# A new instruction list for the first third of a chunked-scan layer followed by a squared-ReLU FFN, on one core

## The chip, the cores and the metric

The kernel runs on one core of a Trainium2 chip. The core has a matrix engine (PE in the profile, with its weight loads shown as PEld), a vector engine (DVE), a scalar engine (ACT), a general engine (POOL, also called GpSimd) and a queue engine that only issues transfers (SP). ACT and POOL issue transfers too. The metric is the device time of one execution in microseconds (us).

## The reference

The program is a gated linear recurrence over a sequence, and then a feed-forward network (FFN) on its output. There are 4 batches, 8 heads, 768 tokens, head width 32 and state width 16.

```python
log_a = np.log(np.clip(a, 1e-06, 1.0))
for c in range(nc):                       # chunks of tokens
    cum = np.cumsum(la, axis=-1)
    L = np.exp(cum[:, :, :, None] - cum[:, :, None, :]) * causal
    M = np.einsum('bhin,bhjn->bhij', Cc, Bc) * L
    y_intra = np.einsum('bhij,bhjd->bhid', M, xc)
    y_inter = np.einsum('bhin,bhnd->bhid', Cc, state) * np.exp(cum)[:, :, :, None]
    y[:, :, sl] = y_intra + y_inter
    state = decay_full[:, :, None, None] * state + np.sum(Bx, axis=2)
x = y.transpose(0, 2, 1, 3).reshape(B * S, H * D)      # 3072 x 256
h = np.maximum(x @ w_in, 0.0)                          # 256 -> 2048
out = (h * h) @ w_out                                  # 2048 -> 256
```

## The kernel before

**Units and blocks.** The kernel replaces the chunks of 32 tokens by chunks of 128 and works on 12 units of 256 tokens each (two chunks): units 0 to 3 are the first third of the four batches, 4 to 7 the second, 8 to 11 the last. The decays are not taken as exponents of sums but as running products: `P` is the running product of `a`, C is multiplied with P, and x with 1/P, so that a causal mask of zeros and ones is all that is left of the decay matrix. Each unit becomes one FFN block of 256 tokens; the blocks are called a to l.

**Everything is ordered by hand.** The string `ORDER` is a list of short names, and the function `one` (line 655) issues what each name stands for. The framework adds the semaphores; it does not reorder. So the place of a name in the list fixes the order of the instructions on each engine, and each engine works through its own instructions in that order. The FFN uses PSUM banks of 2 KB, which `bank` (line 352) hands out in rotation among those not marked busy.

**The names**, with k the unit:

- `fa0`, `fa1`, `la`: loads of `a`. `ldB`, `ldC`, `ldx`: loads of B, C and x of a unit (l and h are the two halves of the heads), with the issuing queue behind the colon (s for SP, a for ACT). `ld4` and so on load all three. `wi0` to `wi3` and `wo0` to `wo3` load a quarter of w_in and w_out each from POOL's queue, 512 KB in the memory, converted on the way.
- `id2:512`: idle products, here two of 128x512, of ones with ones, whose results nobody reads.
- `wm`: a first small copy on ACT, ahead of which the function table is loaded (line 487). `ku ef eb ti pi` build masks and identities on POOL, `jz` clears a buffer for B and C, `mb` builds the causal mask, `hd` and `pk` prepare a small product.
- `sk` (clip and running product of the first third of `a`), `sp` (its transposition on PE), `ps`, `iv1` and `iv` (copy and reciprocals), `su`, `to`, `fq` (the decay totals). `sn`, `p2` and `pq` are the same for the other two thirds of `a`; `sn` is three DVE instructions (lines 468, 469, 532).
- `pc`, `pb`: C times P, and B, into the buffer `jt`. `px`: x times 1/P into `xs`. `tr` and `tc`: transposition of `jt` on PE and copies out of PSUM (units 0 to 3; from unit 4 on a transposing transfer from SP). `mt`: the scores of a unit, into banks 0 to 3.
- `mk`: mask one bank of scores straight from PSUM on DVE (line 229). `sc` and `ms`: copy a bank by ACT (line 234) and mask the copy on DVE or POOL (line 238). A unit has four such steps. `u`: the unit's addition to the state, `us` its copy, `sf` the first state of a unit (line 343), `za zb sa sb` the later states.
- `in`, `ina`, `inb`: products of the masked scores with x. `ca`: product with the state. `t`: copy of the result to `T`, the input of the block (two copies; aa is ACT twice, vv DVE twice).
- `a0` to `a7`: the eight up-products of block a (line 403, four products of 128x256 each), followed by a ReLU on ACT (line 408). `qa0`: the square on DVE (line 414). `A0` to `A7`: the down-products (line 430). The same with b and B, and so on.
- `rg4`: state products, additions and scores of two neighbouring units together, from the middle of the list on. `bk` and `fr` release banks. `gB3`, `gx3`: a memset on POOL that a later load has to wait for.

**Around the change.** The list falls into a front (up to `rg4`) and a steady part, in which up- and down-products alternate and one unit is prepared per block. The diff touches the front of the list and functions that it calls.

Of the kernel before, what the change touches and what calls it, by code (L numbers as in the profile page):

```python
# [30 lines left out]
def kernel(  # L31
# [180 lines left out]
    T = {}  # L212
# [14 lines left out]

    def ph_mask(k, q):
        nc.vector.tensor_tensor(out=live[k]["mts"][:, q].rearrange("p r g i -> p (r g i)"),  # L229
                                in0=pp[:, q, :], in1=mask, op=ALU.mult)  # L230

    def ph_score(k, q):
        sc = big.tile([128, 512], BF16, tag="sc", name=f"sc{k}_{q}")
        nc.scalar.copy(out=sc, in_=pp[:, q, :])
        live[k].setdefault("sc", {})[q] = sc

    def ph_mask_sb(k, q, eng):
        eng.tensor_tensor(out=live[k]["mts"][:, q].rearrange("p r g i -> p (r g i)"),  # L238
                          in0=live[k]["sc"][q], in1=mask, op=ALU.mult)
# [8 lines left out]
    def ph_carry(k, h, begun):  # L248
        for i in range(2):
# [18 lines left out]
    def ph_intra(k, h, begun, qs=range(4)):  # L268
        v = live[k]
        for g in range(2):  # L270
# [8 lines left out]
    def ph_t(k, h, engs=None):  # L279
# [5 lines left out]
        for i, eng in enumerate(engs or (nc.scalar, nc.scalar)):  # L285
            copy(eng, _fap(T[k], i * 64, [[128, 4], [1, 64]]), _fap(pp, h[i] * 512, [[64, 4], [1, 64]]))

# [51 lines left out]
    def ph_sd_first(k):  # L339

        v, b = live[k], UNITS[k][0]
        S_d = spool.tile([128, 256], BF16, tag=f"Sd{b}0", name=f"Sd{k}_0")
        nc.vector.tensor_tensor(  # L343
# [7 lines left out]

    def bank():
        h = next(h for h in turn if h not in busy)
# [4 lines left out]
    def pair():  # L358
        free = sorted((turn.index(h), h) for h in turn if h not in busy)
# [36 lines left out]
    def mm1(blk, fp):  # L396

        h = bank()
        gi, o = group_of(WIN, fp)
        w = w_in_b[gi]  # L400
        for i in range(2):
            for g in range(2):
# [3 lines left out]
                                 start=(g == 0), stop=(g == 1), skip_group_check=True)  # L406
# [49 lines left out]
    with tc.manual_schedule():  # L456
# [131 lines left out]
        def scores(k):  # L588
# [3 lines left out]
            live[k]["todo"] = [0, 1, 2, 3]  # L592
            live[k]["copied"] = []
            live[k]["masked"] = []

        def mask_direct(k):
            q = live[k]["todo"].pop(0)
            ph_mask(k, q)
            busy.discard(q)
# [164 lines left out]
```

## Time and profile before

| | |
|---|---|
| median of three runs | 116.73 us (116.39 to 117.14) |
| the profiled execution | 116.84 us, of which the span of instructions is 115.1 us |
| PE busy | 108.9 us (95% of the span) |
| DVE, ACT, POOL busy | 84.2 us (73%), 76.7 us (67%), 49.8 us (43%) |
| memory read and written | 10.58 MB, 3.15 MB |

The profiled execution has 1.7 us around its span. Busy shares are means over the span; the first 17 us and the rest differ, so that the views by stretch, by time and by chain are read besides.

### The profile page before, as it was taken

Reading aid. Unit: us, or ns where it says so; the run is one execution under the profiler, and the core shown is the slowest. Engines: PE = TensorE matmul, PEld = TensorE weight load, DVE = VectorE, ACT = ScalarE, POOL = GpSimd, SP = SyncE. Lnnn points to the kernel's source line nnn. Section 1 sums busy time; section 2 is a strip of 40 time slices with the busy share of each in tenths; the row PEclk is TensorE's granted clock in tenths of the full one; section 3 lists DMA queues with packets and bytes.
Section 4 is the critical chain, followed back from the end, with each engine's and each line's share of the span. In section 5 each row is a group of like instructions: output and inputs, shape, how many; then the busy total and the mean of one; then the engine's idle time right before and its main releaser. Section 6 shows DMA issues by size and latency. Waiting matters only on the chain.

```text
span 115.1 us, 3998 instructions
## 1 busy us (share of the span) xinstructions
PE 108.9 (95%) x1623; PEld 93.5 (81%) x1623; DVE 84.2 (73%) x187; ACT 76.7 (67%) x161; POOL 49.8 (43%) x102
## 2 busy tenths in 40 slices
PE   7977969999999999999999999999999999999990
PEld 2344749978898989989989989989989899899980
DVE  2469996779599969969965989849668488445530
ACT  0655667865598756787486686786777776876840
POOL 7369972068599457548602669038020020000000
PEclk9999999999999999999999999999999999999999
DMA  1999999989999913935915926623023020020202
GB/s 29 199 196 145 199 203 189 215 167 210 180 191 211 214 24 108 160 89 155 179 46 122 178 97 123 132 95 73 0 100 68 0 100 0 6 91 0 91 0 91
DMA packets 47814, 13.46 MB, mean 117 GB/s; under 512 B 44276, under 2 KB 45876, under 8 KB 47796
## 3 DMA queue, kind: packets, MB, share of 16 engines
q1 hardware_dynamic: 43828, 10.64, 44.8%
q0 software_dynamic: 1664, 2.10, 10.8%
q10 hardware_dynamic: 2304, 0.48, 2.0%
q8 instruction: 12, 0.20, 0.8%
q14 instruction: 6, 0.05, 0.1%
HBM read 10.58 MB, written 3.15 MB: 119 GB/s over the span
## 4 chain that ended last, share of the span: by engine, by line
PE 87%; DMA 6%; POOL 2%; issue 1%; DVE 1%; ACT 1%; ACTq 0%; DVEq 0%
PE pp L430 36%; PE pp L403 36%; PE pp L245 6%; DMA w_out_b<-in_moe_w_out_dram 6%; PE pp L476 4%; PE pp L220 3%; POOL mts L238 1%; PE pp L195 1%; POOL jt L158 1%; PE pp L452 1%; DVE jt L158 0%; DVE Sd L343 0%; ACT bct L208 0%; PE pp L521 0%; ACT osl L722 0%
## 5 line engine op out<-in xcount | busy, mean ns | idle before, releaser
L408 ACT ACTIVATE hb<-pp 128x512 bf16<-128x512 f32 x96 | 55.0, 599 | 24.7 <-PE pp L403 23.1
L430 PE MATMUL pp<-w_out_b,h 128*128 128x256 bf16 (+1 forms) x400 | 54.3, 268 | 0.8 <-DMA w_out_b<-in_moe_w_out_dram 0.8
L414 DVE TENSOR_TENSOR h<-hb 128x512 bf16<-128x512 bf16 x96 | 45.0, 486 | 12.7 <-ACT hb L408 12.3
L403 PE MATMUL pp<-T,w_in_b 128*128 128x256 bf16 x384 | 54.2, 273 | 0.0
L403 PEld LDWEIGHTS <-w_in_b 128*128 128x128 bf16 x384 | 41.4, 114 | 2.2 <-issue 1.0
L430 PEld LDWEIGHTS <-h 128*128 128x128 bf16 x400 | 37.6, 98 | 5.4 <-DVE T L210 1.1
L229 DVE TENSOR_TENSOR mts<-pp,mask 128x512 bf16<-128x512 f32 x45 | 29.6, 677 | 3.3 <-PE pp L220 3.3
L331 POOL TENSOR_TENSOR Sd<-z,Pquad 128x256 bf16<-128x256 f32 x16 | 11.1, 693 | 32.9 <-DVE z L315 25.7
L177 POOL TENSOR_TENSOR xs<-x_nat,Pinv 128x256 bf16<-128x256 f32 (+1 forms) x19 | 14.4, 776 | 5.2 <-DVE Pinv L546 4.6
L158 POOL TENSOR_TENSOR jt<-C_nat,P_sb 128x128 bf16<-128x128 f32 x22 | 9.4, 449 | 1.5 <-ACT P_sb L688 1.0
L476 PE MATMUL pp<-const-bfloat16-1.0 128*128 128x512 bf16 (+2 forms) x19 | 7.3, 516 | 0.8 <-PEq L748 0.8
L315 DVE SCALAR_TENSOR_TENSOR z<-z,Ptot,us 128x64 f32<-128x64 f32 x8 | 2.2, 281 | 6.3 <-ACT us L299 5.4
L437 ACT COPY osb<-pp 128x512 f32<-128x512 f32 x11 | 6.3, 584 | 0.4 <-PE pp L430 0.4
L245 PE MATMUL pp<-mts,xs 64*32 64x128 bf16 x384 | 5.9, 219 | 0.1
L170 POOL CAST jt<-B_nat 128x128 bf16<-128x128 f32 x17 | 5.4, 341 | 1.4 <-DMA B_nat<-in_B_dram 1.4
L220 PE MATMUL pp<-bct 32*64 32x256 bf16 x192 | 5.1, 279 | 0.9 <-DVE bct L210 0.6
L476 PEld LDWEIGHTS <-const-bfloat16-1.0 128*128 128x128 bf16 x19 | 2.2, 122 | 4.0 <-issue 3.7
L245 PEld LDWEIGHTS <-xs 64*32 64x32 bf16 x384 | 4.2, 90 | 0.6 <-issue 0.4
L282 ACT CAST T<-pp 128x512 bf16<-128x512 f32 x7 | 4.1, 592 | 0.4 <-PE pp L245 0.2
L208 ACT CAST T<-pp 128x256 bf16<-128x256 f32 x8 | 2.6, 375 | 2.6 <-PE pp L245 2.6
L245 PE MATMUL pp<-bct,Sd 128*128 128x128 bf16 x40 | 4.2, 220 | 0.0
L220 PEld LDWEIGHTS <-bct 32*64 32x64 bf16 x192 | 2.1, 102 | 2.0 <-issue 0.6
(62 smaller groups left out, 53.4 us busy)
## 6 DMA issues: line engine op xcount, KB each, us to landing
x_nat<-in_x_dram SPq DMA_DIRECT2D x11, 256.0 KB, 3.7
out_dram<-osb SPq DMA_DIRECT2D x11, 256.0 KB, 3.2
B_nat<-in_B_dram SPq DMA_DIRECT2D x11, 128.0 KB, 3.1
C_nat<-in_C_dram SPq DMA_DIRECT2D x11, 128.0 KB, 3.4
w_in_b<-in_moe_w_in_dram POOLq DMA_DIRECT2D x4, 256.0 KB, 6.8
w_out_b<-in_moe_w_out_dram POOLq DMA_DIRECT2D x4, 256.0 KB, 8.2
x_nat<-in_x_dram ACTq DMA_DIRECT2D x2, 128.0 KB, 3.4
bct<-jt SPq DMA_TRANSPOSE x8, 3.6
```

The source lines that it names most:

```text
L158: eng.tensor_tensor(out=_fap(jt[k % 3], 128 + 144 * g, [[384, 2], [32, 4], [1, 16]]), in0=_fap(loaded[k]["C"], 128 * g, [[16, 2], [32, 4], ...
L177: eng.tensor_tensor(out=_fap(xs, 256 * r, [[256, 2 // n], [32, 8], [1, 32]]), in0=_fap(loaded[k]["x"], 32 * r, [[32, 2 // n], [64, 8], [1, ...
L220: nc.tensor.matmul(pp[64 * u:64 * u + 64, q, r * 256:r * 256 + 256], bct[32 * q:32 * q + 32, r, 0, u * 64:u * 64 + 64], _fap(bct[32 * q:32 ...
L229: nc.vector.tensor_tensor(out=live[k]["mts"][:, q].rearrange("p r g i -> p (r g i)"), in0=pp[:, q, :], in1=mask, op=ALU.mult)
L245: nc.tensor.matmul(dst, w, v, start=bool(need), stop=False, skip_group_check=True, **({} if pos is None else {"tile_position": pos}))
L331: nc.gpsimd.tensor_tensor(out=_fap(S_d, 0, [[128, 2], [32, 4], [1, 32]]), in0=_fap(z, 0, [[32, 2], [0, 4], [1, 32]]), in1=_fap(Pquad, 4 * ...
L403: nc.tensor.matmul(pp[:, h, i * 256:(i + 1) * 256], _fap(w, g * w.shape[2] + (o // 2) * 512 + 2 * (o % 2) + i, [[4, 128]]), T[blk][:, g].r ...
L408: nc.scalar.activation(out=hb.rearrange("p i t -> p (i t)"), in_=pp[:, h, :], func=AF.Relu)
L414: nc.vector.tensor_tensor(out=h2, in0=hb, in1=hb, op=ALU.mult)
L430: nc.tensor.matmul(dst, h2[:, i, r * 128:(r + 1) * 128], w_out_b[gi][:, 2 * o + i, c0:c1], start=first, stop=(fp == 7 and i == 1), skip_gr ...
L437: nc.scalar.copy(out=osb, in_=pp[:, 6 if blk == 1 else 7, :])
L476: nc.tensor.matmul(pp[:, h, 0:int(cols)], ones_b[:, 0:128], ones_b[:, 0:int(cols)] if dep is None else dep, start=True, stop=True, skip_gr ...
```

## The change

`ORDER` is rewritten from its start up to `rg4`; from there on it is the same. In the new front:

- the idle products ahead of the FFN are 28 instead of 19, with more of them between `sp` and the first `ca`, and of other sizes;
- on ACT, `wm` stands ahead of the loads of the lower halves of C and x of unit 0 (`ldC0:l`, `ldx0:l`), behind them before;
- `jz0` goes from DVE to POOL, `jz1` and `jz2` trade places, `pbl0` and `pbh0` trade engines (DVE and POOL for POOL and ACT);
- `in0` stands ahead of `mt1`; `sf0` and `sf2` are on ACT (four activations each) instead of DVE;
- POOL issues `wo0`, `wi2` and `wi3` ahead of `px1`; `px1` stood between `wo0` and `wi2`;
- after the masks of unit 1 come `sf1`, then `sn`; `p2` stands behind `a3`;
- four up-products of block b are issued ahead of `A0`; none before. Some up-products are issued in halves (`a0:0`, `a0:1`), each half two of the four products;
- on DVE instead of POOL or ACT: `pb2`, `px2`, `tc3:1`, `px4`, `pc5`, `pb5`; `t1` goes from DVE to ACT; unit 2 is masked by `mk` alone, unit 3 has one `sc` and `ms`; `pb3` goes from ACT to POOL;
- the gate `gx3` behind `wo2` replaces `gB3` at the start, and SP loads C of unit 2 ahead of B.

The tuple `HALF` is empty, so the branches for it aren't taken. The quarters of the weights stay as they were.

```diff
-        id3:512 fa1:a la fa0:s ku ef ldx0:h:a eb id2:512 ti id1:512 gB3 pi ldB0:l:a hd ldC0:l:a ldB0:h:s ldC0:h:s
-        ldx0:l:a wm jz0:v mb jz1:v ldB1:s id3:512 sk pbh0:a id2:512 pk pbl0:p wi0 sp pc0:v ldC1:s trB0 wi1 su iv1:0:8
-        trC0 tcC0:0:v tcB0:2:a id1:512 tcC0:1:a ps pb1:a to px0:v jz2:v mt0 id1:512 u0:67 ldx1:s pc1:p fq sc0 mk0
-        id1:512 mk0 ms0:p tr1 tc1:1:v sc0 tc1:0:a sf0 mt1 ldB2:s wo0 ldC2:s ms0:v ldx2:s id1:384 in0 ca0 iv:8:16
-        id3:512 px1:p t0:aa id1:256 mk1 a0 a1 mk1 mk1 mk1 u1 ina1 inb1 sn1 us0 sf1 qa0 a3 ldC3:s wi2 fr p2 wi3 ca1
-        qa1 wo1 pc2 pb2:a t1:vv us1 iv:32:64 a2 zb0 qa2 zb1 A0 ldB3:s wo2 ldx3:s b3 qb3 b0 pq b2 b1 tr2 wo3 sb1 qa3
-        qb0 A1 b5 b4 qb1 qb2 qb5 tc2:1:v qb4 tc2:0:a a5 B0 b6 B1 a7 qa5 iv:16:32 px2 a6 mt2 B3 A2 sc2 u2 b7 us2 pb3:a
-        pc3 mk2 qa6 px3 mk2 A5 ms2:v mk2 ld4 qb6 sf2 a4 qa7 B5 pc4 A6 A3 ld5 pb4 ina2 inb2 tr4 ca2 t2:aa tr3 B4 B2
-        tc3:0:a tc3:1:a u3:45 qb7 ld6 ld7 mt3 qa4 B6 mk3 mk3 mk3 mk3 us3 c4 c5 c0 A4 A7 B7 c6 qc0 za3 qc4 c1 qc5 qc6
-        sa3 px4 qc1 pc5 pb5 bk c2 rg4 tr5 C0 mk4 mk4 qc2 c7 qc7 sb0 c3 qc3 d2 d1 C5 za4 afC2 d0 C1 px5 C4 qd2 zb3 C6
+        la jz2:v fa1:a id1:384 id1:512 id2:512 jz0:p fa0:s ldB0:h:s id2:512 ldx0:h:a ldC0:h:s ku ef ldB0:l:a ti wm
+        id1:512 ldC0:l:a ldx0:l:a id2:512 sk id1:128 eb id1:128 sp mb pbl0:v hd id1:256 id1:384 id1:256 iv1:0:8 pi
+        pbh0:p ldB1:s id1:384 wi0 ldC1:s ps id1:512 ldx1:s trB0 pk jz1:v pc0:v tcB0:2:a id1:384 id1:128 su trC0
+        tcC0:0:a to iv:8:16 tcC0:1:v pb1:a id2:512 wi1 px0:v fq mt0 id2:512 ldC2:s pc1 sc0 sc0 mk0 id1:384 u0:67
+        id2:512 ms0:p mk0 wo0 wi2 wi3 ms0:v tr1 us0 ldB2:s in0 id1:128 px1:p tc1:0:a tc1:1:v mt1 id2:512 sf0:a ldx2:s
+        ca0 t0:aa a0:0 mk1 a0:1 mk1 ldC3:s mk1 mk1 a1 u1 sf1 us1 a2:0 a2:1 ina1 inb1 wo1 sn1 a3:0 ca1 t1:aa ldB3:s
+        a3:1 p2 b1:0 b2:0 b1:1 qa3 qa1 qa0 pc2:p b0 b3 iv:16:32 b2:1 qb1 A0 wo2 gx3 iv:32:64 ldx3:s zb1 fr qb0 a5 A1
+        b5 wo3 B0 pb2:v B1 b4:0 pq qa5 qb2 b4:1 a7:0 qb3 a6 pc3 pb3:p a7:1 tr2 tc2:1:a px2:v B3 b6 A3 qb4 qb5 tc2:0:v
+        B2 u2@45 mt2 qa2 A2 ld4 qa6 sb1 qa7 B5 us2 mk2 b7 px3:p mk2 sf2:a pc4 A5 mk2 a4 A6 mk2 tr3 ca2 ina2 inb2
+        tc3:0:a t2:aa tc3:1:v mt3 ld5 qb6 B4 pb4:p sc3 u3:45 qa4 qb7 B6 mk3 us3 c4 tr4 c0 px4:v mk3 ld6 B7 pc5:v za3
+        A4 qc4 mk3 ms3:v qc0 c6 sa3 c5 A7 pb5:v c1 bk zb0 ld7 qc5 c2 qc1 qc6 rg4 tr5 C0 mk4 mk4 qc2 c7 qc7 sb0 c3 qc3
...
-    def ph_sd_first(k):
+    def ph_sd_first(k, eng=None):
...
+        if eng is nc.scalar:
+            for q in range(4):
+                nc.scalar.activation(out=_fap(S_d, 32 * q, [[128, 2], [1, 32]]),
+                                     in_=_fap(pp, v["h"][0] * 512 + 256, [[32, 2], [1, 32]]),
+                                     func=AF.Copy, scale=Pquad[:, total(0, b, 0), q:q + 1])
+            v["S"] = [None, S_d]
+            return
...
+    def mm1(blk, fp, part=None):
+
+        h = opened.pop((blk, fp)) if part == 1 else bank()
...
-            for g in range(2):
+            for g in (0, 1) if part is None else (part,):
...
-                                 start=(g == 0), stop=(g == 1), skip_group_check=True)
+                                 start=(g == 0 and (part is None or i == 0)), stop=(g == 1), skip_group_check=True)
+        if part == 0:
+            opened[(blk, fp)] = h
+            busy.add(h)
+            return
+        busy.discard(h)
```

More of the change, by code (lines that the diff above doesn't have):

```diff
@@ L286, in ph_t, with ph_t_half @@
             copy(eng, _fap(T[k], i * 64, [[128, 4], [1, 64]]), _fap(pp, h[i] * 512, [[64, 4], [1, 64]]))
+    def ph_t_half(k, h, g, eng):
+        if k not in T:
+            T[k] = tpool.tile([128, 2, 2, 2, 64], BF16, tag="T", name=f"T{k}")
+        d = h[1] - h[0]
+        copy(eng, _fap(T[k], 256 * g, [[128, 2], [64, 2], [1, 64]]),
+             _fap(pp, h[0] * 512 + 128 * g, [[64, 2], [512 * d, 2], [1, 64]]))
     state = {}
@@ L350 @@
     busy = set()
+    forced = []
     def bank():
-        h = next(h for h in turn if h not in busy)
+        h = forced.pop(0) if forced else next(h for h in turn if h not in busy)
+        assert h not in busy
         turn.remove(h)
@@ L358, in pair @@
     def pair():
+        if forced:
+            return tuple(bank() for _ in range(2))
         free = sorted((turn.index(h), h) for h in turn if h not in busy)
@@ L591, in scores, with read_out @@
             busy.update(range(4))
-            live[k]["todo"] = [0, 1, 2, 3]
+            live[k]["todo"] = [(g, p) for g in range(2) for p in range(2)] if k in HALF else [0, 1, 2, 3]
             live[k]["copied"] = []
             live[k]["masked"] = []
+        def read_out(k, q):
+            if k not in HALF:
+                busy.discard(q)
+            elif q[0]:
+                busy.difference_update((2 * q[1], 2 * q[1] + 1))
         def mask_direct(k):
@@ L598, in mask_direct @@
             ph_mask(k, q)
[L599 removed]
+            read_out(k, q)
             live[k]["masked"].append(q)
@@ L622, in intra @@
             v = live[k]
+            if k in HALF:
+                gs = {"": (0, 1), "a": (0,), "b": (1,)}[part]
+                assert all((g, p) in v["masked"] for g in gs for p in range(2))
+                ph_intra(k, v["h"], v["begun"], range(4), gs)
+                return
             qs = v["masked"][{"": slice(0, 4), "a": slice(0, 2), "b": slice(2, 4)}[part]]
```

68 lines of the change are left out of this document (45 added, 23 removed).

## The prediction

> **What bounds the kernel now.** I read the chain of waits first, in order of time, then the busy time by stretch. The columns of the chain are start, length (us) and what it was.
>
> ```profile
> 0.85 4.85 PE pp L476 x11
> ...
> 10.33 6.49 DMA w_out_b<-in_moe_w_out_dram
> 16.82 0.14 issue
> 16.96 0.60 PE pp L430 x4
> 17.56 1.75 PE pp L403 x16
> ```
>
> ```profile
> 16.96:112.19 95.23, 95.10 (x1424) 86.01 (x1424) 72.07 (x156) 68.09 (x136) 37.16 (x70) 1.00 0.53 110
> 20.00:35.00 15.00, 14.88 (x241) 12.80 (x244) 12.13 (x25) 10.91 (x26) 9.22 (x18) 1.00 1.08 193
> ```
>
> The second fence has a stretch, its length, the busy time of PE, PEld, DVE, ACT and POOL, the granted clock, the DMA share and GB/s. From 16.96, where the first down-product A0 starts, to 112.19 PE is busy 95.10 of 95.23 us. So the kernel is a front of 17 us in which PE mostly waits, and then 95 us of PE work without a hole. What A0 waited for is the first quarter of w_out, issued at 10.33 and landed 6.49 us later. The time changes by two things alone: how early PE becomes dense, with how much useful work done before, and what holes the dense part gets or loses. One hole is there to lose:
>
> ```profile
> 26.35 1.47 PE L430 MATMUL pp<-w_out_b,h 128*128 128x256 bf16 x12
> 27.94 0.27 PE L245 MATMUL pp<-mts,xs 64*32 64x128 bf16 x5
> ```
>
> A product of 128x256 takes 1.75/16 = 0.109 us in a row, four of them 0.44 (one name such as `a0`). Twelve from 26.35 issue until 27.66; the next is at 27.94, so 0.28 us are lost.
>
> **The change part by part.** From `rg4` on the list is the same, and the useful PE work of the front is the same set. I walk the new front, with the durations of before.
>
> *Until the first scores.* The 11 first idle products now have 4736 columns instead of 5632. At the early rate (4.85/11 = 0.44 us for 512) they end at about 4.9 instead of 5.7. That gains nothing, as `sp` waits for the scan of `a`, and the transfer of `a` keeps its place. What moves is C:
>
> ```profile
> 2.44 0.53 ACTq L125 DMA_DIRECT2D C_nat<-in_C_dram  x1
> 3.01 0.52 ACTq L125 DMA_DIRECT2D x_nat<-in_x_dram  x1
> 3.56 1.28 ACT L487 ACT_TABLE_LOAD   x1 [3.56 <-issue]
> 4.85 0.19 ACT L487 COPY warm<-warm 128x2 bf16<-128x2 bf16 x1
> ```
>
> The table load and copy (1.28 + 0.19) now stand ahead of these two issues, so C's lower half is issued at 2.44 + 1.5 = 3.9, x's at 4.5: the first x is not moved up for this half, but back. The time from issue to landing of this C transfer was
>
> ```profile
> DMA to landing us min/median/max: 3.2/3.2/3.2
> ```
>
> and so it lands at 7.1 instead of 5.6. Below, the first products with C (6.31) did not wait for it; now they start at 7.1.
>
> ```profile
> 6.31 0.49 DVE L158 TENSOR_TENSOR jt<-C_nat,pp 128x128 bf16<-128x128 f32 x2 [0.96 <-PE pp L452]
> ...
> 7.77 0.68 DVE L177 TENSOR_TENSOR xs<-x_nat,Pinv 128x512 bf16<-128x512 f32 x1
> 8.48 0.38 DVE L685 MEMSET jt<- 128x384 uint32 x1
> ...
> 11.00 2.42 DVE L229 TENSOR_TENSOR mts<-pp,mask 128x512 bf16<-128x512 f32 x4
> 13.34 0.37 DVE L468 TENSOR_SCALAR a_cl<-a_nat 128x128 f32<-128x128 f32 x1
> 13.74 0.43 DVE L469 TENSOR_TENSOR_SCAN cp<-a_cl,const-float32-0.0 128x128 f32<-128x128 f32 x1
> 14.20 0.84 DVE L532 TENSOR_SCALAR pick_p<-pick,cp 128x16 f32<-128x16 f32 x1
> 14.96 0.41 DVE L343 TENSOR_TENSOR Sd<-pp,Pquad 128x256 bf16<-128x256 f32 x1
> ```
>
> ```profile
> 7.47 0.38 PE L476 MATMUL pp<-const-bfloat16-1.0 128*128 128x512 bf16 x1
> 8.09 0.42 PE L220 MATMUL pp<-bct 32*64 32x256 bf16 x16 [0.24 <-ACT bct L208]
> ```
>
> From those products to the scores (8.09) it took 1.78 us, with the reciprocal and `su` in between, which now come earlier. I take 1.5, so the scores of unit 0 start at 8.6, 0.5 late. The memset of `jt` (0.38), `pbl0` and `hd`, new on DVE ahead of the products with C, lie beside the wait for C; without it they would cost at most 0.4.
>
> *The idle products* between `sp` and `trC0` hold 2304 columns. At the early rate that is 4.5 x 0.44 = 1.98 us, at the later one 4.5 x 0.22 = 0.99 (twice 0.109 for 512 columns; the single one at 7.47 took 0.38 with its way through the array, where the early ones come every 0.44). They start at about 6.2 and are over at 7.2 or 8.2; `trC0` can start at 7.6. So they cost between 0 and 0.6. I take 0, as the rate was already the later one at 7.47, and keep 0.6 for the range. The granted clock is 1.00 in every row and does not show this. The Trainium skill, "TensorE: Matmul & The Clock Gate", Part 1, says that PE starts at half rate and is released after a window of about 3.4 us of sustained activity, a window that runs freely; by that rule the pause of the new list between 4.9 and 5.6 can fall into the window and put the release off, the idle products meant to keep the rate up would then run at half of it ahead of real work, and the sum would be 0.6 higher.
>
> *Masks, T and the products with x.* POOL is next:
>
> ```profile
> 8.24 0.82 POOL L158 TENSOR_TENSOR jt<-C_nat,P_sb 128x128 bf16<-128x128 f32 x2 [1.00 <-ACT P_sb L688]
> 9.04 0.23 POOL L527 TENSOR_TENSOR Pquad<-Ptot,quad 128x32 f32<-128x32 f32 x1
> 9.24 1.15 POOL L238 TENSOR_TENSOR mts<-sc,mask 128x512 bf16<-128x512 bf16 x1
> 10.33 0.60 POOL L143 DMA_DIRECT2D w_out_b<-in_moe_w_out_dram  x1
> 11.18 1.04 POOL L177 TENSOR_TENSOR xs<-x_nat,Pinv 128x512 bf16<-128x512 f32 x1 [0.24 <-DVE Pinv L546]
> 12.17 1.47 POOL L139 DMA_DIRECT2D w_in_b<-in_moe_w_in_dram  x2
> ```
>
> Its mask came 1.15 after the scores started and took 1.15: now 9.75 to 10.9. `in0` follows at 10.95, as before (10.94). `mt1` now stands behind `in0` and an idle product, at 11.35 instead of 10.31: 1.0 late. Its four masks (2.42) run from 11.8 to 14.2. Meanwhile POOL issues `wo0` (0.60) and `wi2`, `wi3` (1.47) from 10.9 to 13.0 and only then makes xs of unit 1 (1.04): 14.0, against 12.2 before. `u1` and `ina1`, on PE in order behind it, wait for 14.0 and 14.2; so both delays end together. `sf1` follows (0.41) to 14.7 or 14.9, then `sn`: from its first to the end of its last instruction 1.70 us (13.34 to 15.04), so 16.5, then the sums of `p2` on PE, and the first product of b at about 16.65. T1, copied by ACT after `ca1`, is there before. a0 to a3, units 0 and 1 and `p2` are then done: exactly what was done at 16.96. **PE gets dense 0.3 us earlier.** The four activations for `sf0` on ACT have no row; between 0.19 (the small copy) and 0.41 (the DVE instruction) each, they take 0.8 to 1.6. I take 0.8, hidden by the idle products ahead of `ca0`; at 1.6 T0 is 0.5 later, and PE, which waits for 14.0 anyway, has room for a0 and a1 (0.9).
>
> *The weights.* The third quarter of w_in, issued at 12.17, landed after
>
> ```profile
> DMA to landing us min/median/max: 6.7/6.7/6.7
> ```
>
> at 18.9. POOL's transfers land one after the other, and DMA is full (1.08 of a share in the row of 20 to 35), so issuing it at 11.5 behind the same predecessors moves it little. In the new list a5, which needs it, is behind b1, b2, b0, b3 and A0: 16.7 + 5 x 0.44 = 18.9. This caps what an earlier T could bring: **dense from 16.7**, a gain of 16.96 - 16.7 = 0.26. A0's weights are there at 16.8, before its turn at 18.4.
>
> *The hole at 27.7* came, by the chain, from Sd of unit 2 on DVE behind a slow square. Now it is made by ACT, and `tr3` fills PE ahead of `ca2`. I take the whole 0.28 as gained; its other end is 0.
>
> *DVE in the dense part* is what covers all this. New on it between 20 and 35: px2 and px4 at 0.68 each, pc5 0.49, pb2 and pb5 (casts never seen on DVE: from 0 to the 0.49 of pc5; I take that, it is the same shape) 0.98, one copy for unit 3 (from 0 to a mask's 2.42/4 = 0.6; I take 0.4), less Sd 0.41: 2.8 us. It was idle 15 - 12.13 = 2.87 there. It just fits; what does not fit comes out as late masks, up to 0.5 by my count. POOL is relieved of as much, and that helps DVE:
>
> ```profile
> L414 DVE TENSOR_TENSOR h<-hb x18: 412/437/1077, 17.5 to 34.8; 128x512 bf16<-128x512 bf16 x18
> ```
>
> The same square takes 412 to 1077 ns. The Trainium skill, "SBUF — State Buffer", section "SBUF: two separate sides", says that a DVE instruction with two SBUF inputs and a POOL one exclude each other for their whole length; by this row it may well be so, the squares would gain from the moved work, and the 0.5 would go to 0.
>
> *Sum*, against the profiled 116.84 (0.1 above the median 116.73, so it is a typical one): - 0.26 - 0.28 = - 0.54, **116.3 us**.
>
> **The rivals.**
>
> *A, the cover is gone.* The idle products run at the early rate (+ 0.6), or DVE, full, takes the place of the hole (+ 0.5). Either gives 116.8 to 116.9, both 117.4: no change that can be told. For it speaks that DVE has 0.07 us to spare; against it, that the slow squares should get fewer.
>
> *B, slower.* C's lower half lands late. It now goes out behind the table load, while SP's queue is full: the load of B of unit 1, which waited for `a`, goes earlier.
>
> ```profile
> SPq L125 <- DMA a_nat<-in_a_dram: 1.2, 1, 1.2
> ```
>
> The transfer of x of unit 1 in that crowd landed after
>
> ```profile
> DMA to landing us min/median/max: 5.5/5.5/5.5
> ```
>
> instead of 3.2. At 5.5 C lands at 9.4, 2.3 later than I count; scores, masks of unit 1 and `sn` all shift, and the time is 116.3 + 2.3 = 118.6. From 4.9 us to landing on, the kernel is over 1% slower than before (1.17 + 0.54 = 1.7 us of shift). Against it: C is on ACT's queue and half as large as x of unit 1.
>
> *C, faster by over 1%.* The 1.2 us of SP's wait are used: everything is loaded up to 1.2 earlier, C and the weights too, and the two caps (18.9 and xs of unit 1 at 14.0) move together. Dense from 15.9, and the hole: - 1.06 - 0.28, 115.5. Against it: POOL's 2.1 us of issuing stand ahead of `px1` whatever lands.
>
> *D, the change does not do what it says*: a5 waits for its weights at 18.9 wherever b is, and `ca2` for POOL instead of DVE. 116.8, inside A.
>
> **How the numbers follow.** My forecast, 115.9 to 116.7, has 0.42; A with D 0.23, inside 1% for its most part; B 0.2; C 0.15. A measurement here tells about 1% (1.17 us) from no change. So faster 0.15, same 0.63, slower 0.22 (B and the worst of A). The range goes from a little below C, 115.3, to 118.1: above lies the worse half of B, below the better third of C.
>
> **What would show it.** C's products at 7.1 and the scores of unit 0 at 8.6; `mt1` near 11.4; xs of unit 1 at 13.0 to 14.0; the first product of b at 16.7 and a5 at 18.9; no pause near 28; DVE over 14 of 15 us busy between 20 and 35. I am wrong if the scores of unit 0 start after 9.5 (B), if PE has holes behind 20 with masks or squares as their ends (A), or if a weight quarter lands over 0.5 us earlier (C).

## The result and the profile after

The changed kernel takes 117.78 us (median of five, 117.57 to 117.97) against 116.73 (five, 116.39 to 117.14): a ratio of 1.0087, interval 1.0059 to 1.0116. It is slower by 1.05 us, where 116.3 was forecast: a loss of under 1%, larger than the uncertainty, on the other side than forecast. The profiled execution took 117.57, its span 115.7 us, against 116.84 and 115.1. So 0.6 of the 1.05 lies inside the span; the rest is around it (0.1) and in which executions were profiled. Executions of one kernel differ, in part by how long PE runs at half its rate in the front, so that a ratio compares the quicker executions of both kernels (up to 1.5% above the quickest), while a median is of all of them.

First the chain that ended last, as before: start, length, what it was.

```profile
0.81 0.74 SPq L598
...
1.61 3.01 DMA a_nat<-in_a_dram
...
5.55 0.43 PE pp L497 x8
5.98 0.88 PE pp L521 x5
...
8.42 0.68 DVE xs L180
9.10 1.28 DVE mts L242 x2
10.38 0.94 DVE mts L257
...
11.37 0.41 PE pp L264 x29
11.77 0.16 PE pp L521
11.94 0.41 PE pp L223 x16
...
12.95 1.89 DVE mts L242 x3
...
14.88 0.61 PE pp L443 x4
...
15.49 0.28 ACT us L322
...
15.81 0.47 PE pp L264 x29
16.27 0.34 PE pp L443 x2
```

No transfer of weights is on it any more. Before, the chain left POOL's mask for w_out and came to PE at 16.96; now it runs through `a`, five idle products (5.98), x, the masks of unit 0 on DVE, `in0` (11.37), one idle product (L521), the scores of unit 1 (11.94), their masks, a2 (14.88), the copy `us` on ACT (15.49) and `ina1` (15.81). The first product of b comes at 17.51, with the same work done as before at 16.96: 0.55 late.

The dense part is as long as it was. Before, and after, from there to `rg4`:

```profile
16.96:34.71 17.75, 17.64 (x247) 15.58 (x248) 13.96 (x31) 13.06 (x31) 9.54 (x19) 1.00 1.10 192
```

```profile
17.51:35.29 17.78, 17.60 (x248) 15.61 (x248) 15.30 (x42) 13.37 (x33) 5.66 (x13) 1.00 1.10 186
```

PE's busy time is 17.64 of 17.75 us before and 17.60 of 17.78 after, so the old hole is paid back by a new one ahead of the scores of unit 3 and by smaller ones:

```profile
29.79 0.42 PE L223 MATMUL pp<-bct 32*64 32x256 bf16 x16 [0.18 <-DVE h L459]
```

0.55 + 0.03 = 0.58, and the spans differ by 0.6. The moved work on DVE did not make the stretch longer:

```profile
20.00:35.00 15.00, 14.82 (x223) 12.88 (x222) 12.68 (x35) 10.98 (x26) 5.08 (x12) 1.00 1.11 186
```

```profile
L459 DVE TENSOR_TENSOR h<-hb x19: 373/418/512, 17.7 to 34.9; 128x512 bf16<-128x512 bf16 x19
```

DVE is busy 12.68 of 15 us (12.13 before; over 14 was forecast), as no square takes longer than 512 ns any more, where the longest took 1077. The row of the new hole names a square, the forecast's sign of rival A, in small.

What stands on the chain, with its neighbours, from the timeline of all engines:

```profile
9.89 1.15 POOL L257 TENSOR_TENSOR mts<-sc,mask 128x512 bf16<-128x512 bf16 x1
...
10.30 1.02 DVE L257 TENSOR_TENSOR mts<-sc,mask 128x512 bf16<-128x512 bf16 x1
...
11.24 0.34 DVE L213 COPY bct<-pp 128x384 bf16<-128x384 bf16 x1
...
11.88 0.93 ACT L371 ACTIVATE Sd<-pp,Pquad 128x64 bf16<-128x64 f32 x4 [0.61 <-PE pp L264]
...
12.69 0.88 ACT L211 CAST T<-pp 128x256 bf16<-128x256 f32 x2
...
13.62 1.03 PE L443 MATMUL pp<-T,w_in_b 128*128 128x256 bf16 x8 [0.46 <-ACT T L211]
...
14.25 1.09 ACT L453 ACTIVATE hb<-pp 128x512 bf16<-128x512 f32 x2 [0.68 <-DVE mts L242]
...
15.81 0.47 PE L264 MATMUL pp<-mts,xs 64*32 64x128 bf16 x32 [0.34 <-ACT us L322]
```

DVE's mask of unit 0 takes 1.02 us, against 0.41 before. Before, it ran behind POOL's mask; now it runs beside it and ends 0.28 behind POOL's. The other profiles show that this is no accident: in ten with this order of the masks, DVE's begins at another point of POOL's, takes 0.53 to 1.02 us, and ends 0.28 or 0.29 behind POOL's in each. So it waits for POOL's mask, whatever its own length. Two things wait for it: `in0`, and the copy of `tc1` (11.24) that the scores of unit 1 need. Behind `in0` a second line starts: Sd on ACT, which begins when `in0` has ended, then T of unit 0, then a0 at 13.62 (12.20 before). a0, a1 and `u1` are over at 14.88, the masks of unit 1 at 14.83: both lines end in front of a2.

### The profile page after: what moved, and what is told of

Read it like the earlier page. It is cut to its first block, busy times and chain, and to the rows that moved or that the text cites. A ratio compares the mean times of both kernels' runs of the same rounds, so it can differ in the third digit from the quotient of the medians.

```text
span 115.7 us, 4014 instructions
## 1 busy us (share of the span) xinstructions
PE 109.6 (95%) x1630; PEld 94.0 (81%) x1632; DVE 83.6 (72%) x193; ACT 78.2 (68%) x165; POOL 46.9 (40%) x98
## 4 chain that ended last, share of the span: by engine, by line
PE 86%; DVE 6%; DMA 3%; issue 1%; ACT 1%; SPq 1%; ACTq 0%; DVEq 0%
PE pp L475 37%; PE pp L443 37%; PE pp L264 6%; PE pp L223 3%; DVE mts L242 3%; DMA a_nat<-in_a_dram 3%; PE pp L198 1%; PE pp L521 1%; DVE mts L257 1%; PE pp L497 1%; SPq L598 1%; DVE xs L180 1%; DVE bct L213 1%; DVE cp L514 0%; ACT bct L211 0%
## 5 line engine op out<-in xcount | busy, mean ns | idle before, releaser
L459 DVE TENSOR_TENSOR h<-hb 128x512 bf16<-128x512 bf16 x96 | 43.4, 471 | 13.1 <-ACT hb L453 12.8
L180 POOL TENSOR_TENSOR xs<-x_nat,Pinv 128x256 bf16<-128x256 f32 (+1 forms) x16 | 12.2, 781 | 0.0
L161 POOL TENSOR_TENSOR jt<-C_nat,P_sb 128x128 bf16<-128x128 f32 x20 | 8.5, 445 | 6.6 <-DMA C_nat<-in_C_dram 6.6
L521 PE MATMUL pp<-const-bfloat16-1.0 128*128 128x512 bf16 (+3 forms) x26 | 7.7, 428 | 1.2 <-PEq L813 0.8
L521 PEld LDWEIGHTS <-const-bfloat16-1.0 128*128 128x128 bf16 x28 | 2.7, 114 | 4.0 <-issue 3.6
L173 POOL CAST jt<-B_nat 128x128 bf16<-128x128 f32 x17 | 4.7, 304 | 1.1 <-DMA B_nat<-in_B_dram 1.1
L264 PEld LDWEIGHTS <-Sd 128*128 128x128 bf16 x40 | 3.1, 98 | 0.8 <-ACT Sd L371 0.5
L211 ACT CAST T<-pp 128x256 bf16<-128x256 f32 x10 | 3.4, 376 | 0.3
```

The costliest lines, as they stand in the source:

```text
L161: eng.tensor_tensor(out=_fap(jt[k % 3], 128 + 144 * g, [[384, 2], [32, 4], [1, 16]]), in0=_fap(loaded[k]["C"], 128 * g, [[16, 2], [32, 4], ...
L180: eng.tensor_tensor(out=_fap(xs, 256 * r, [[256, 2 // n], [32, 8], [1, 32]]), in0=_fap(loaded[k]["x"], 32 * r, [[32, 2 // n], [64, 8], [1, ...
L264: nc.tensor.matmul(dst, w, v, start=bool(need), stop=False, skip_group_check=True, **({} if pos is None else {"tile_position": pos}))
L459: nc.vector.tensor_tensor(out=h2, in0=hb, in1=hb, op=ALU.mult)
L521: nc.tensor.matmul(pp[:, h, 0:int(cols)], ones_b[:, 0:128], ones_b[:, 0:int(cols)] if dep is None else dep, start=True, stop=True, skip_gr ...
```

## The experiments

Three readings were at stake. **F**: the chain just read makes the loss. **G**: the clock makes it: the pause between the idle products and `prep_p` (the product of `sp`) puts the release off. **C**: the transfer of C behind the table load. Later: is it the dense part, or the weights? The kernels of a group ran on one chip beside the kernel before, the groups on different chips (its medians 116.4 to 117.6). Ratios are to the kernel before. The changed kernel itself ran beside its variants in the second group only; elsewhere a ratio can only be held against its 1.0087 above and 1.0119 there.

### First: one step of the front each

`us` of unit 1 behind T1:

```diff
-a1 u1 sf1 us1 a2:0 a2:1 ina1 inb1
+a1 u1 sf1 a2:0 a2:1 ina1 inb1
...
-ca1 t1:aa ldB3:s
+ca1 t1:aa us1 ldB3:s
```

> The new list with one edit: us1 (the copy of unit 1's state addition, on ACT) stands behind t1 instead of ahead of ina1. Theory F (the loss is the chain of the front: ina1 waits for us1, which waits on ACT behind two ReLUs of block a until 15.76 us): ina1 starts at about 15.4 instead of 15.81, the first product of b at 17.1 instead of 17.51, time 117.4 us. Rival D (the loss is in the dense part, where DVE has more to do): no change, 117.8. Rival A (idle products delay PE's real work): no change, 117.8.

118.34 us, ratio 1.006 [1.0018, 1.0103]. The wait ahead of `ina1` is gone and the first b comes 0.28 earlier, then it is given back (PE's timeline):

```profile
15.53 0.47 PE L264 MATMUL pp<-mts,xs 64*32 64x128 bf16 x32
...
17.23 1.91 PE L443 MATMUL pp<-T,w_in_b 128*128 128x256 bf16 x16
...
23.65 0.60 PE L475 MATMUL pp<-w_out_b,h 128*128 128x256 bf16 x4 [0.24 <-DVE h L459]
```

The page names the square; the second quarter of w_out, which B3 needs, landed at 23.6 in this execution (21.3 in the changed kernel's).

Sd on ACT ahead of `in0`:

```diff
-tr1 us0 ldB2:s in0 id1:128 px1:p tc1:0:a tc1:1:v mt1 id2:512 sf0:a ldx2:s
+tr1 us0 sf0:a ldB2:s in0 id1:128 px1:p tc1:0:a tc1:1:v mt1 id2:512 ldx2:s
```

> The new list with one edit: sf0 (four activations on ACT) stands ahead of in0, as it did before, so that it doesn't read a bank that in0 still writes. Theory F: sf0 runs at 10.3 instead of 11.9, T of unit 0 is ready at 12.8 instead of 13.6, the ReLUs of a0 and a1 leave ACT before u1 is done, ina1 then waits for the masks of unit 1 (14.8) alone, and p2 for its scan (16.3): first product of b at 16.6 instead of 17.5, time 116.9 us. If the wait of sf0 for in0 is not through the bank, no change, 117.8. Rivals A and D: 117.8.

117.83 us, ratio 1.0051 [1.0006, 1.0096]. The profiled execution is one in which the idle products run at half rate:

```profile
6.37 1.68 PE L521 MATMUL pp<-const-bfloat16-1.0 128*128 128x256 bf16 x5
...
10.28 0.42 PE L223 MATMUL pp<-bct 32*64 32x256 bf16 x16
...
14.98 1.03 PE L443 MATMUL pp<-T,w_in_b 128*128 128x256 bf16 x8 [0.46 <-ACT T L211]
15.94 0.25 PE L264 MATMUL pp<-xs,jt 64*32 64x64 bf16 x16
16.45 0.60 PE L443 MATMUL pp<-T,w_in_b 128*128 128x256 bf16 x4 [0.26 <-DVE mts L242]
...
18.87 1.36 PE L443 MATMUL pp<-T,w_in_b 128*128 128x256 bf16 x11
```

The five idle products behind `prep_p` take 1.68 us here and 0.94 in the changed kernel's profile, and the scores of unit 0 start at 10.28 instead of 8.56. Counted from these scores, a0 comes after 4.70 us instead of 5.06, the first b after 8.59 instead of 8.95: 0.36 won, and then the masks of unit 1 hold a2 (0.26).

Three masks of unit 0 on DVE from PSUM, in place of the one beside POOL:

```diff
-sc0 sc0 mk0 id1:384 u0:67 id2:512 ms0:p mk0 wo0 wi2 wi3 ms0:v tr1
+sc0 mk0 mk0 id1:384 u0:67 id2:512 ms0:p mk0 wo0 wi2 wi3 tr1
```

> The new list with one edit: unit 0 is masked three times straight from PSUM and once by POOL from a copy (before and after: twice and twice), so that the DVE mask that took 1.02 us beside POOL's mask is gone. Theory F: the last mask of unit 0 ends at 10.95 instead of 11.32, mt1 starts 0.35 earlier (11.5), the rest of the front moves with it, time 117.4 us. If the 1.02 us are not from POOL running beside it, the third direct mask is as slow and nothing changes. Rivals A and D: 117.8.

118.93 us, ratio 1.0116 [1.0062, 1.0169]. Again a half-rate execution (scores at 10.17). `tr1` now waited 0.66 for the bank that the third mask holds; the first b came 9.10 behind the scores. Nothing won: one wait was exchanged for another.

No idle products between `sp` and a0 (ten places, of which two stand here):

```diff
-hd id1:256 id1:384 id1:256 iv1:0:8
+hd iv1:0:8
...
-mt1 id2:512 sf0:a
+mt1 sf0:a
```

> The new list without the 17 idle products behind sp. Theory F: none of them stood in the way of real work that was ready (PE waited for others at their end), so 117.8 us, if the clock holds without them. Rival A: the idle products cost PE 0.3 to 0.6 us, time 117.2 to 117.5. If the idle products are what keeps TensorE at its full rate, the products of the front run at half of it and the time is 118.3 or more.

120.94 us, ratio 1.0291 [1.0237, 1.0344]. By stretch (the granted clock is the third number from the end):

```profile
8.00:11.00 3.00, 1.95 (x38) 1.25 (x39) 1.59 (x4) 1.61 (x6) 1.50 (x4) 0.50 1.17 175
...
17.00:20.00 3.00, 3.00 (x54) 1.75 (x48) 1.22 (x4) 2.14 (x6) 0.50 (x2) 0.50 1.04 142
```

Without them PE falls back to half its clock from 8 to beyond 20 us. The idle products do their work; whether they also cost something can't be read from this run.

### Second: the first pause filled, xs first

> The changed kernel once more, to stand beside the next three. Both theories: 0.5 to 1.2 us above the kernel before, ratio 1.004 to 1.010. Theory F (a longer chain in the front) has all executions alike, with the scores of unit 0 at 8.6 and the first product of b at 17.5. Theory G (the pause ahead of prep_p lets the clock's release slip in some executions) has some of them about 1.5 us longer, with the scores at 10.2.

The changed kernel again: 118.74 us, ratio 1.0119 [1.0039, 1.02], executions from 117.47 to 120.55. Its profile repeats the first (scores 8.71, a0 13.67, b 17.56).

768 more columns ahead of `sp`:

```diff
-eb id1:128 sp mb
+eb id1:128 id1:512 id1:256 sp mb
```

> 768 more columns of idle product (0.66 us at the early rate) fill PE's pause between the last early idle product and prep_p; all else stays. Theory G: no execution has its release put off, the scores of unit 0 start at 8.3 to 8.7 in the profile, the median falls 0.2 to 0.6 below the changed kernel's and the slowest execution by over 1 us. Theory F: nothing in the chain is touched, so within 0.2 of the changed kernel, first product of b at 17.5.

118.44 us (118.17 to 120.23), ratio 1.0183 [1.0122, 1.0244]. The median is 0.3 lower, as G had it, but the slowest execution is only 0.3 quicker than the slowest above and the quickest 0.7 slower: G is not borne out, and not refuted either. For the slowest execution, the profiled one, also differs at its other end: its last two stores, of 64 KB each, landed 3.6 us after their issue, 1.7 in the changed kernel's profile. So 1.9 us of its span of 118.5 have nothing to do with the front (the same stores took up to 3.5 in two later profiles, and 2.3 in that of the run with `us` behind T1). Its front, at full rate, shows another cause, on DVE:

```profile
7.78 0.49 DVE L161 TENSOR_TENSOR jt<-C_nat,pp 128x128 bf16<-128x128 f32 x2 [1.18 <-DMA C_nat<-in_C_dram]
```

The lower half of C took 3.46 us instead of 1.95 (the run above) and held everything 0.9 up. That is reading C, in one execution. In the changed kernel's profile C's products (6.76) did not wait for C at all; they followed the memset of `jt` on DVE (6.33, 0.38 us).

xs of unit 1 right behind POOL's mask, with the first two edits (that of `us` isn't shown again):

```diff
-ms0:p mk0 wo0 wi2 wi3 ms0:v tr1 us0 ldB2:s in0 id1:128 px1:p tc1:0:a tc1:1:v mt1 id2:512 sf0:a
+ms0:p px1:p mk0 wo0 wi2 wi3 ms0:v tr1 us0 sf0:a ldB2:s in0 id1:128 tc1:0:a tc1:1:v mt1 id2:512
```

> xs of unit 1 is made on POOL right behind its mask, ahead of the weight issues; the four ACT copies for Sd stand ahead of in0; us of unit 1 stands behind T1. Theory F: u1 and ina1 no longer wait for xs and us, ina1 by about 14.6 instead of 15.81, first product of b at 16.4 to 16.9 instead of 17.51, and the time 0.5 to 0.9 below the changed kernel's, unless the weight quarters, issued about 1 us later, hold A0 or a5 (then the gain comes back at 19 to 24 us and the time is within 0.3). Theory G: the profile's front shifts as a whole only; executions vary by 1.5 us as before.

118.09 us, ratio 1.0124 [1.0054, 1.0195]:

```profile
13.52 1.03 PE L443 MATMUL pp<-T,w_in_b 128*128 128x256 bf16 x8 [0.46 <-ACT T L211]
...
15.00 0.60 PE L443 MATMUL pp<-T,w_in_b 128*128 128x256 bf16 x4 [0.26 <-DVE mts L242]
...
17.22 1.91 PE L443 MATMUL pp<-T,w_in_b 128*128 128x256 bf16 x16
...
22.42 1.06 PE L443 MATMUL pp<-T,w_in_b 128*128 128x256 bf16 x8 [0.24 <-DMA w_in_b<-in_moe_w_in_dram]
```

The first b comes 8.44 behind the scores instead of 8.95, and the gain is given back: PE waits at 22.4 for the last quarter of w_in, issued 1.3 us later than in the changed kernel. The same with the filled pause:

> The two edits together. F and G both true: 0.7 to 1.3 us below the changed kernel, that is at or below the kernel before (ratio 0.995 to 1.001), first product of b at 16.4 to 16.9, scores of unit 0 at 8.3 to 8.7. If only F holds it equals the run with xs first, if only G holds the run without the first pause.

118.92 us, ratio 1.0196 [1.012, 1.0272]. Here the second quarter of w_out, issued 0.4 later than in the changed kernel and landed 10.6 us after that instead of 7.3, held PE for 1.5 us:

```profile
25.04 0.60 PE L475 MATMUL pp<-w_out_b,h 128*128 128x256 bf16 x4 [1.50 <-DMA w_out_b<-in_moe_w_out_dram]
```

### Third: C ahead of the table load, and the front of before

```diff
-ti wm id1:512 ldC0:l:a ldx0:l:a id2:512
+ti ldC0:l:a ldx0:l:a wm id1:512 id2:512
```

> The changed kernel with C's lower half and x's issued on ACT ahead of the table load, as in the kernel before. Theory C (this transfer starts the front late): C's products at 6.1 to 6.3 instead of 6.76, scores of unit 0 at 7.9 to 8.2 instead of 8.56, first product of b at 16.9 to 17.1 instead of 17.51, and the time 0.3 to 0.6 below the changed kernel's, with less spread between executions, as a late landing of this half no longer reaches the scores. Theory F (the loss is made behind the scores, in the order of masks, xs and us): the scores move, but the first product of b stays within 0.2 of 17.5, and so does the time.

118.94 us, ratio 1.0136 [1.0054, 1.0218]. The three quickest spans (115.4 to 115.8) are some 0.4 below those of the changed kernel in the second group (115.8 to 116.2), but at most 0.2 below those of its first runs (115.6 to 115.7), each on another chip; the others reach 120. The profiled one, with the transfer of `a` late and idle products at half rate (1.68 us), had its scores at 10.81, and here too C's products followed the memset on DVE without a wait for C. A gain from C is not shown.

The list of before up to A0, then the order and engines of the changed one:

```diff
-la jz2:v fa1:a id1:384
+id3:512 fa1:a la fa0:s
...
-ca1 t1:aa ldB3:s a3:1 p2
+t1:vv us1 iv:32:64 a2 zb0 qa2 zb1 ldB3:s
 b1:0 b2:0 b1:1
```

> The list of the kernel before up to its first down-product A0, and from there the order and the engines of the changed one. If all of the loss is made in the front (theories C, F): no slower than the kernel before; as b1, b2, b0, b3 now stand ahead of A0, they can start when T of unit 1 is there, at about 16.7, in place of the wait for w_out to 16.96: 0 to 0.3 below the kernel before, ratio 0.997 to 1.000. If the new dense part loses too (rival A: DVE): slower than the kernel before by 0.3 or more, with holes between 20 and 35.

117.93 us, ratio 1.0004 [0.9945, 1.0064]: **with the front of before, the loss is gone.** The interval reaches 0.6%, so a smaller loss of the new dense part could still hide in it; the stretch to `rg4` above, 17.78 us instead of 17.75, leaves no room for one. So the loss is made in the front. Five of the twelve executions had a granted clock above 0.99. The profiled one, at 0.971, shows where the others lose:

```profile
5.00:8.00 3.00, 1.73 (x18) 1.08 (x18) 1.79 (x7) 1.45 (x7) 1.92 (x3) 0.99 0.91 165
8.00:11.00 3.00, 2.61 (x40) 1.30 (x41) 2.27 (x5) 2.16 (x8) 2.58 (x5) 0.50 1.13 171
11.00:14.00 3.00, 2.78 (x54) 1.38 (x55) 3.00 (x8) 0.70 (x2) 2.06 (x4) 0.50 1.13 180
```

PE was busy 1.73 of the 3 us from 5 to 8, and then the clock falls to half until 14; a0 came at 14.48 instead of 12.20. So the clock costs time in the front of before. Two attempts to fill its pauses, first ahead of A0, in the kernel before:

```diff
-wi2 fr p2 wi3
+wi2 fr id1:256 p2 wi3
...
-us1 iv:32:64 a2 zb0
+us1 iv:32:64 a2 id1:512 id1:512 id1:512 zb0
```

> The kernel before with four idle products in its two waits ahead of A0 (256 columns ahead of p2, three of 512 behind a2). Theory G (a wait of about 0.8 us ahead of A0 makes the clock fall back for a stretch in some executions): executions with a granted clock of 0.97 become rare, the median of all executions falls by 0.2 to 0.8, the quickest ones stay. Without G: no change, at most 0.1 slower.

117.84 us, ratio 1.0119 [1.0058, 1.018]. The place was wrong, and the idle products waited themselves:

```profile
16.98 0.81 PE L477 MATMUL pp<-const-bfloat16-1.0 128*128 128x512 bf16 x3 [1.18 <-ACT hb L409]
17.63 0.60 PE L431 MATMUL pp<-w_out_b,h 128*128 128x256 bf16 x4
```

They write a PSUM bank that a ReLU was still reading, and A0 stood behind them: 17.63 instead of 16.96. Then in the hybrid, with one of 512 columns in place of the three:

> The hybrid (front of before, dense part of the changed kernel) with two idle products in the waits ahead of b. Theory G: the quick executions as in the hybrid, those at a lower granted clock rarer; 0 to 0.6 below the kernel before. Without G: as the hybrid.

117.53 us, ratio 1.0056 [1.002, 1.0092]; five of twelve executions still at a clock of 0.985 or less, and the idle product ahead of b waited 0.93 in the same way.

### Fourth: the scores of unit 1 first, and the pauses of the right stretch

F was narrowed to F2: the late scores of unit 1 are the step.

```diff
-fq mt0 id2:512 ldC2:s pc1
+mt0 id2:512 ldC2:s pc1 fq
...
-u0:67 id2:512 ms0:p mk0 wo0 wi2 wi3 ms0:v tr1 us0 ldB2:s in0 id1:128 px1:p tc1:0:a tc1:1:v mt1 id2:512
+u0:67 ms0:p mk0 tr1 id2:512 tc1:1:v tc1:0:a wo0 wi2 wi3 mt1 ms0:v us0 ldB2:s in0 id1:128 px1:p id2:512
```

> The changed kernel with the way to the scores of unit 1 as before: C's products of unit 1 ahead of Pquad on POOL, the transposes ahead of the idle products, the copies of them and the scores ahead of the last mask and in0. Theory F2 (late scores of unit 1 make b late): those scores at 10.8 to 11.2 instead of 11.87, their masks over at 13.7 to 14.1 instead of 14.82, first product of b at 16.9 to 17.2 instead of 17.51, time 0.3 to 0.5 below the changed kernel. Rival (xs and us of unit 1 hold ina1 in any case): b stays within 0.2 of 17.5.

120.53 us, ratio 1.0273 [1.0212, 1.0333]: F2 falls.

```profile
9.59 0.42 PE L224 MATMUL pp<-bct 32*64 32x256 bf16 x16
...
12.42 0.42 PE L224 MATMUL pp<-bct 32*64 32x256 bf16 x16
...
13.46 0.41 PE L265 MATMUL pp<-mts,xs 64*32 64x128 bf16 x29 [0.45 <-DVE mts L258]
...
15.70 1.03 PE L444 MATMUL pp<-T,w_in_b 128*128 128x256 bf16 x8 [0.46 <-ACT T L212]
```

The scores of unit 1 did come earlier, 2.83 behind those of unit 0 instead of 3.31. But `in0` moved behind the late mask, and a0 came 6.11 behind the scores instead of 5.06. The second line, through T of unit 0, had been hidden by an equal first one. That it became this long is again DVE's mask: it took 1.12 us.

The same, with `us` of unit 1 behind T1 and `ina1` ahead of a2, and then C ahead of the table load besides:

```diff
-u1 sf1 us1 a2:0 a2:1 ina1 inb1
+u1 sf1 ina1 inb1 a2:0 a2:1
...
-t1:aa ldB3:s
+t1:aa us1 ldB3:s
```

> The same, and us of unit 1 behind T1, ina1 and inb1 ahead of a2. F2: ina1 at 14.2 to 14.6 instead of 15.81, first product of b at 16.2 to 16.7, that is 0.8 to 1.3 earlier; the time 0.3 (if the weight quarters hold A0, a5 or B3 later) to 1.2 (if they don't) below the changed kernel, at best level with the kernel before or 0.3 below it. Rival: first b at 17 or later.

> The same as the last, and C's lower half issued ahead of the table load. The quickest executions 0.2 to 0.5 below those of the last, first product of b at 15.8 to 16.5 where the clock is released early; without an effect of C as the last.

121.10 us (ratio 1.0265 [1.0169, 1.0361]) and 122.03 us: the same fault, and `ina1` now waited 0.6 for Sd of unit 1.

The hybrid, with idle products in the pauses between 6.2 and 8.1 us:

```diff
-sp pc0:v ldC1:s trB0 wi1 su
+sp id1:256 pc0:v ldC1:s trB0 id1:512 wi1 su
...
-pb1:a to px0:v
+pb1:a id1:384 to px0:v
```

> The hybrid with 1152 columns of idle product in the three pauses between 6.2 and 8.1 us. Theory G: executions with a granted clock of 0.97 go from about half to at most one in four, the median of all falls by 0.5 to 1.0 below the hybrid's, to 116.9 to 117.4, below the kernel before's median on the same chip. Without G: as the hybrid, or up to 0.2 slower.

116.72 us (116.12 to 117.39) beside 117.22 for the kernel before: all twelve executions had a clock of 0.996 or more, of the kernel before nine of 17. The ratio, 0.9976 [0.9939, 1.0013], does not tell the two apart: what is won are the executions that fall back. In the profile PE is busy 2.61 of the 3 us from 5 to 8, and the clock stays:

```profile
5.00:8.00 3.00, 2.61 (x38) 1.50 (x36) 1.85 (x6) 1.79 (x9) 2.08 (x4) 1.00 1.02 187
8.00:11.00 3.00, 2.37 (x90) 1.32 (x75) 2.97 (x9) 1.68 (x6) 2.75 (x6) 1.00 1.03 168
```

### Fifth: both lines ahead of a2

The first two edits of the first group together; the weight issues stay:

```diff
-tr1 us0 ldB2:s in0
+tr1 us0 sf0:a ldB2:s in0
...
-u1 sf1 us1 a2:0
+u1 sf1 a2:0
...
-t1:aa ldB3:s
+t1:aa us1 ldB3:s
```

> The changed kernel with the four ACT copies for Sd of unit 0 ahead of in0 and us of unit 1 behind T1; the weight issues stay. Theory T (PE's work behind a0 is one row without room: first b = a0 + 3.55, or + 3.9 with the wait for us): from the scores of unit 0 to a0 4.7 us instead of 5.06, from a0 to the first b 3.5 to 3.7 instead of 3.89, so that with the scores at 8.56 b starts at 16.8 to 17.0 instead of 17.51; the quickest executions 0.3 to 0.7 below the changed kernel's 117.5, about 117.0, if the weights aren't what holds next. Rival (weights): b as early, but the time within 0.2 of the changed kernel, with waits for a weight quarter at 18 to 25 us.

117.52 us, ratio 1.0126 [1.0054, 1.0198]. In the profile x of unit 0 landed late (scores at 9.22); from the scores it is 4.88 to a0 and 8.57 to the first b, where the changed kernel has 8.95. So 0.38 was won of the 0.5 to 0.7 expected: a2 waited 0.26 for the masks of unit 1, the other line. No weight quarter is waited for. The three quickest executions took 116.9 to 117.1, the quickest of the changed kernel 117.5, but on another chip; the ratio shows no gain. T, that PE's work behind a0 is one row, holds as far as the rows go.

T of unit 1 earlier, in the hybrid with filled pauses:

```diff
-wi3 ca1 qa1 wo1 pc2 pb2:a t1:vv us1
+wi3 ca1 t1:av us1 qa1 wo1 pc2 pb2:a
```

> The hybrid with filled pauses, T of unit 1 copied by ACT and DVE at once and right behind ca1, ahead of the squares and casts. First product of b at 15.4 to 15.7 instead of 16.07 in the profile; 0.2 to 0.6 below the hybrid with filled pauses (116.1 to 116.5 in the median, ratio to the kernel before 0.990 to 0.996), or nothing, if a5 then waits for the third quarter of w_in, which lands at 18.3 to 18.9.

116.64 us beside 116.43, ratio 1.0025 [0.9984, 1.0065]: no gain is shown. In the profile a2 waited 1.03 us for the second quarter of w_in, which took 8 us to land.

## Why the prediction was wrong

**Right**: the scores of unit 0 at 8.56 (8.6 forecast), but by luck: C's products came at 6.76, not 7.1, as DVE's own work and not C's landing set them, and from there to the scores it took 1.80, not 1.5; the two errors cancel. Right without luck: the idle products behind `prep_p` at the full rate in the profile; POOL's mask at 9.89 to 11.04 and xs of unit 1 at 14.07 (9.75 to 10.9, 14.0). The old hole went. DVE did not become the bound, for the reason given against rival A, though over 14 of 15 us busy were forecast.

**The step that failed** is the walk from the masks of unit 0 to the first product of b, forecast 16.65, measured 17.51. The working had `ina1` at 14.2, and `sn` as the last to end. Measured, `ina1` came at 15.81. Of these 1.6 us, 0.6 are the masks of unit 1, over at 14.83 instead of 14.2. Half of that is DVE's mask of unit 0, a term that the working put at nothing: it had `in0` follow POOL's mask "as before", but before it followed DVE's, which stood behind POOL's:

```profile
10.51 0.41 DVE L238 TENSOR_TENSOR mts<-sc,mask 128x512 bf16<-128x512 bf16 x1
10.94 0.45 PE L245 MATMUL pp<-mts,xs 64*32 64x128 bf16 x32
```

In the new order DVE's mask ended 0.28 behind POOL's, which ended 0.14 later than forecast; so `in0` came at 11.37 instead of 10.95, and the scores of unit 1 behind it at 11.87 instead of 11.35. The next 0.6 to 0.7 are a2, which stands ahead of `ina1` and needs the bank that the last mask frees; I had let `ina1` follow the masks directly. 0.3 are `us` of unit 1, a copy on ACT behind two ReLUs (over at 15.34), which began when a2 had ended too (15.49) and which I had not looked for. `sn`, a term of 1.70, took 0.94, and was not what held; from `ina1` PE has work in a row to the first b, by chance also 1.70 us. 14.2 + 1.70 = 15.9 left 0.75 of room below 16.65, and 1.6 - 0.75 = 0.86 is the miss.

**The four activations for Sd**: taken at 0.8 and hidden. They took 0.93, but began only when `in0` had ended, and T of unit 0 stood behind them on ACT. The sentence "PE has room for a0 and a1" was the mistake: in seven profiles, the changed kernel's among them, the first b follows a0 by 3.89 or 3.90 us, and in the four with `us` of unit 1 behind T1 and a2 ahead of `ina1` still by 3.54 to 3.70. There was no room.

**The weights' cap**: a5 was forecast to wait until 18.9; it started at 19.69 and waited for nothing, so it was not a bound here. Other quarters held PE in three of the five variants in which b came earlier (0.24 us in two, 1.5 in one), and none in the other two.

**The hole**: 0.28 was counted as gained. It went, but the new order has one of its own, 0.18 ahead of the scores of unit 3, and smaller ones, and the dense part is 17.78 instead of 17.75 long. With the first miss, (17.51 - 16.7) + (0.28 + 0.03) = 1.12: from - 0.54 to + 0.58.

**Rival A** was priced at 0.6 and is real, but larger: in four of the thirteen profiles with the new front's start (the 0.94 or 1.68 us of the five idle products tell them apart) the release came late, and the scores of unit 0 at 10.2 to 10.8, 1.6 us or more late. The Trainium skill, "TensorE: Matmul & The Clock Gate", Part 1, says that the release comes after a freely running window of activity; these executions agree with it. But filling the pause ahead of `sp` did not show fewer of them in time, so that this pause is the cause stays open. **Rival B** in small happened too: in two profiles DVE waited 1.18 and 0.98 us for C's half.

**What stays open**: the hybrid shows that the loss is in the front, and the rows show where: the two lines ahead of a2, `us`, and the row of work behind a0. Moving these brought the first b nearer to the scores of unit 0 by 0.36 to 0.51 us in five profiles, but no variant of the new front was shown to be quicker in time. That DVE's mask waits for POOL's stands on the ten profiles; it was not tried alone.

## What to carry to other kernels

When work is moved ahead in a list, look at each in-order engine for what now stands in front of the critical item, and price an instruction by a row in which the same neighbours run. Two lines of equal length hide each other: mending one wins little, and a reorder that helps one can cost on the other. A filler instruction needs a free bank, and its place is in the pauses ahead of the point at which the clock falls, which a profile of a disturbed execution shows.

## What the hardware showed unexpectedly

- The front of before, in the hybrid's first profile, loses half its clock from 8 to 14 us, and 1152 columns of idle product in the pauses from 6.2 to 8.1 kept it in all of twelve executions. By the Trainium skill, "TensorE: Matmul & The Clock Gate", Part 1, the clock falls back after an idle window of about 3.4 us. Here 1.27 us without work out of 3, in pauses of 0.7 and less, were enough; the measurement decides. How much is allowed stays open: in two profiles of variants of the new front (with the scores of unit 1 first, and with both lines ahead of a2) PE had no work for 1.36 us of the same three, and the granted clock stayed at 1.00.
- DVE's mask of two SBUF inputs took 0.41 us beside POOL's issue of w_out, and up to 1.02 beside POOL's mask, ending 0.28 or 0.29 behind it in all ten profiles. The Trainium skill, "SBUF — State Buffer", section "SBUF: two separate sides", says that such an instruction and one of POOL exclude each other; the rows agree. But in the run with the scores of unit 1 first it took 1.12 with only POOL's issues of weights beside it, and ended 0.29 behind the first of two issues of w_in (12.41, 0.70 us), which that does not explain.
- Weight quarters landed 4.7 to 10.9 us after their issue, in kernels that differ in the order of a few names, and the last stores of 64 KB 1.7 to 3.6 us after theirs.
